# Attention scores of six tiles in one phase, values in one phase, and one score tile copied out of PSUM by VectorE

## The chip, the cores and the metric

The kernel runs on one core of a Trainium2 chip. The metric is the device time of one execution in microseconds (us); lower is better. The core has a matrix engine (TensorE; PE in the profile, with its weight loads listed apart as PEld), three engines for elementwise work (VectorE = DVE, ScalarE = ACT, GpSimd = POOL), a queue that issues the DMAs (SyncE = SP), a large on-chip memory (SBUF), and PSUM, the memory that matmuls write to. In this kernel PSUM is cut into three buffers of 128 x 1024 float32 (the pool `ps_2`) and two of 128 x 512 (`ps_1`).

## The reference, cut to what matters

```python
def _attn_ref(q, k, v):                      # batch 8, heads 12, sequence 448, head size 64
    scores = matmul(q, k.T) / sqrt(64) - log(448)
    attn = 1 / (1 + exp(-scores))            # a sigmoid, no softmax: no sum over a row
    return matmul(attn, v)

def _moe_ref(x, w_in, w_spatial, b_spatial, w_out):
    h = maximum(x @ w_in, 0);  u, g = halves of h
    g = (g - mean(g)) / sqrt(var(g) + 1e-6)
    g = einsum('ts,bsd->btd', w_spatial, g) + b_spatial
    return (u * g) @ w_out
```

Inputs and outputs are float32. The attention output of all heads, side by side, is `x`.

## The kernel before, in words

The eight batch elements are handled in four blocks of two (`m` = 0 to 3). A block first does the attention of its two batch elements, then the gated MLP: `gate_values` (tiles `pv`), `spatial` (`pg`), `gated` (`pu`) and `output` (`po`). The attention of the next block starts a little inside the MLP of the block before: its first four score tiles stand ahead of the last three `output` calls.

**Units and pairs.** A unit `(b, hp)` is one batch element and two heads; a block has 12 units, handled as six pairs (an even unit `n` and an odd unit `n + 1`). Two heads of 64 rows fill the 128 partitions, so every score or value step is two matmuls, one per head (`j` = 0, 1), in different halves of the matrix engine, which run at the same time. Keys are cut into three full tiles of 128 and one short tile of 64. A pair has seven score tiles: `evens` 0, 1, 2 (the even unit's full tiles), 3 (`NFULL`, the short tiles of both units in one), and `odds` 4, 5, 6 (the odd unit's).

**Scores** (`attention_scores`, tiles `psc`). A full tile is three products of split float32 numbers (`TERMS`: high by high, low by high, high by low), so six matmuls (L245; 64 rows by 128 columns of the engine). The short tile is done in plain float32 (L227; 64 by 64). Each `psc` takes one `ps_2` buffer; ScalarE applies the sigmoid on the way out of PSUM into SBUF (L253, tiles `at`). The high and low parts (`qks`) are made by `attention_splits` (L100 and L101): in block 0 the high part is made by ScalarE, later by VectorE; the low part always by VectorE. The very first pair (`direct`) is scored in plain float32, without splits.

**Values** (`attention_values`, tiles `pav`, one `ps_1` buffer per unit). For every `at` tile the product with `v` in plain float32 (L283): full tiles use 128 rows by 64 columns of the engine, the short tile 64 by 64, four matmuls for both units and both heads. When a unit is complete, ScalarE writes its high part to `x_s` (L289) and VectorE subtracts to get the low part (L262).

**The order of the work** is that in which the code is written: every engine executes its instructions in program order (`in_program_order`). For a pair inside a block, `attention` wrote: short tile of this pair; DMA loads; `evens` scores; values of the previous pair's `odds`; `odds` scores; splits of the next pair; values of this pair's `evens` and short tile.

**Weights.** In block 0 the float64 weights are loaded and converted between the attention steps. `load_weights(k)` runs k steps of the generator `weight_steps`: a DMA of a raw weight tile two tiles ahead (L159; `wraw`; up to the thirteenth in three buffers with the tag `tmp`), for the first spatial tile also a DMA of the bias (`b_bc`, L167), and VectorE work: three operations (L113, L124, L127), two (L129, L132), and a cast with a subtraction (L180, L181). A spatial weight tile (`w_sp`) needs the last two only. The loads of a raw tile wait until the buffer's earlier tile has been read, and they stand in SP's queue with the loads of q and k (L200, `raw`, three buffers) and of v (L205).

Of the kernel before, what the change touches and what calls it, by code (L numbers as in the profile page):

```python
# [8 lines left out]
F32 = mybir.dt.float32  # L9
F32R = mybir.dt.float32r  # L10
# [4 lines left out]
P = 128  # L15
# [20 lines left out]
def attn_gmlp_kernel(  # L36
# [25 lines left out]
    nc = tc.nc  # L62
# [138 lines left out]
        loaded[b, hp] = raw  # L201

    def value_loads(b, hp):
        vt = work.tile([P, 2 * NFULL + 1, P], F32, tag="v", name=f"v_{b}_{hp}", bufs=3)
        nc.sync.dma_start(vt, v[b, hp // 2])  # L205
        values[b, hp] = vt

# [2 lines left out]
    def attention_splits(b, hp):  # L210
        raw = loaded[b, hp][:, :PART]
        s = work.tile([P, 2, 2 * S], F32R, tag="split", name=f"qks_{b}_{hp}", bufs=3)[:, :, :PART]
        split(s[:, 0], s[:, 1], raw, nc.vector.tensor_copy if b > 1 else nc.scalar.copy)
        parts_of[b, hp] = s
# [2 lines left out]

    TILES = 2 * NFULL + 1

    def attention_scores(b, hp, t):  # L220
        psc = banks(f"psc_{b}_{hp}_{t}")
        if t == NFULL:
            for odd in range(2):
                raw = loaded[b, hp + odd]
                for j in range(2):
                    rows = slice(j * D, (j + 1) * D)
                    nc.tensor.matmul(  # L227
                        psc[odd * HALF : (odd + 1) * HALF, j, :S],
                        raw[rows, PART:],
                        raw[rows, FULL:PART],  # L230
                        start=True,
                        stop=True,
                    )
        else:
            unit = b, hp + t // (NFULL + 1)
            k = t % (NFULL + 1) * P
            if unit in parts_of:
                s = parts_of[unit]
                ops = [(s[:, a], s[:, e]) for a, e in TERMS]
            else:  # L240
                ops = [(loaded[unit], loaded[unit])]
            for i, (st, mv) in enumerate(ops):
                for j in range(2):
                    rows = slice(j * D, (j + 1) * D)
                    nc.tensor.matmul(  # L245
                        psc[:, j, :S],
                        st[rows, k : k + P],
                        mv[rows, FULL:PART],
                        start=i == 0,
                        stop=i == len(ops) - 1,  # L250
                    )
        at = work.tile([P, 2, 512], F32, tag="big", name=f"at_{b}_{hp}_{t}", bufs=7)[:, :, :S]
        nc.scalar.activation(at, psc[:, :, :S], AF.Sigmoid, bias=bias_s, scale=QK)  # L253
        return at

    pav_of = {}
# [4 lines left out]
        while late:  # L261
            nc.vector.tensor_sub(*late.pop(0))  # L262

    last = (NFULL, TILES - 1)

    def attention_values(b, hp, t, at):
        vt = values[b, hp]
        for odd in range(2):
            if t == NFULL:
                rows = slice(odd * HALF, (odd + 1) * HALF)  # L270
            elif (t > NFULL) == odd:
                rows = slice(0, P)
            else:
                continue
            unit = b, hp + odd
            start = t == odd * NFULL
            stop = t == last[odd]
            if start:
                pav_of[unit] = ps_1.tile([P, 512], F32, tag="ps1", name=f"pav_{b}_{hp + odd}")
            pav = pav_of[unit]  # L280
            for j in range(2):
                heads = slice(j * D, (j + 1) * D)
                nc.tensor.matmul(pav[heads, :S], vt[rows, t, heads], at[rows, j], start=start, stop=stop)  # L283
        for odd in range(2):
            if t == last[odd]:
                sl = slice((b % 2) * S, (b % 2 + 1) * S)
                x = x_s[:, :, hp + odd, sl]
                pav = pav_of.pop((b, hp + odd))[:, :S]
                nc.scalar.copy(x[:, 0], pav)  # L289
                late.append((x[:, 1], pav, x[:, 0].bitcast(F32)))  # L290
# [14 lines left out]
    def gate_values(m, ts):  # L305
# [26 lines left out]
            nc.vector.tensor_scalar_sub(rv[:, i], rv[:, i], mv[:, i, 0:1])  # L332
        load_weights(1)
        for i, t in enumerate(ts):
            vn = work.tile([P, 2, 512], F32R, tag="big", name=f"vn_{m}_{t}", bufs=7)
            if t != NFULL:
                parts = [(vn[:, 0], vn[:, 1], slice(0, P))]
            else:

                a, c = slice(0, HALF), slice(HALF, P)  # L340
                parts = [(vn[a, 0], vn[c, 0], a), (vn[c, 1], vn[a, 1], c)]
            for hi, lo, rows in parts:
                nc.vector.tensor_scalar_mul(hi, rv[rows, i], rstd[rows, i : i + 1])  # L343
                nc.vector.scalar_tensor_tensor(  # L344
                    lo,
                    rv[rows, i],
                    rstd[rows, i : i + 1],
                    hi.bitcast(F32),
                    op0=ALU.mult,
                    op1=ALU.subtract,  # L350
                )
            vns[t] = vn
            if t % 2 == 0:
                load_weights(1)
# [85 lines left out]
    def ahead(f, n, end=len(units)):  # L440
        if n < end:
            f(*units[n])
# [8 lines left out]
    def attention(m):  # L451

        first, end = 2 * NHP * m, 2 * NHP * (m + 1)
        ats = {}
        budget = [NYIELDS if m == 0 else 0]

        def weigh(n):
            n = min(n, budget[0])
            budget[0] -= n
            load_weights(n)  # L460

        def scores(n, ts):
            for t in ts:
                ats[n, t] = attention_scores(*units[n], t)

        def vals(n, ts):
            for t in ts:
                attention_values(*units[n], t, ats.pop((n, t)))
            late_splits()

        short, evens, odds = (NFULL,), tuple(range(NFULL)), tuple(range(NFULL + 1, TILES))
        for n in range(first, end, 2):
            direct = n == 0

            def loads():
                ahead(attention_loads, n + 3, end)
                ahead(value_loads, n + 2, end)
                ahead(attention_loads, n + 4, end)

            if direct:  # L480
                scores(n, evens + short)
            else:
                scores(n, short)
                loads()
                scores(n, evens)
            if n == first:
                yield
                if not direct:
                    attention_splits(*units[n + 1])
            else:  # L490
                vals(n - 2, odds)
                weigh(3)
            scores(n, odds)
            if direct:
                loads()
            ahead(attention_splits, n + 2, end)
            ahead(attention_splits, n + 3, end)
            vals(n, evens + short)
            weigh(3 + (n + 2 == end))
        vals(end - 2, odds)  # L500

    start_loads(0)
    load_weights(1)
# [84 lines left out]
```

## Time and profile before

| | |
|---|---|
| time, median of 3 runs | 692.84 us (692.56 to 693.68) |
| time of the profiled execution | 692.46 us |
| its span, first to last instruction | 690.7 us |
| TensorE busy | 680.6 us, 99% |
| VectorE busy | 282.1 us, 41% |
| ScalarE busy | 250.2 us, 36% |
| sigmoids (L253) | 168, mean 1008 ns |
| granted TensorE clock | 1.0 throughout |

How to read it: the span is cut by engine, busy time is the union of an engine's instructions. Matmuls overlap and their ends are modelled, so a matmul's length is not what it adds to the time; the distance between the starts of successive matmuls is. "The chain of waits" is the work that ended last, followed back from the end: each row has a start, a length, an engine and a line. A row of the timeline has start, length, engine, line, operation, tiles, and in brackets how long the engine had been idle and who ended that.

### The profile page before, as it was taken

The page shows a single profiled execution, that of the slowest core. Times are in us where ns is not written, and L with a number is a line of the kernel's source. Part 1 is how long each engine was busy: PE and PEld are TensorE (multiplying, and loading weights), DVE is VectorE, ACT ScalarE, POOL GpSimd, SP SyncE. Part 2 cuts the span into 40 slices and gives each one's busy share as a digit, 9 for nine tenths or more (in the row PEclk, how much of TensorE's full clock was granted, in tenths as well). Part 3 has the DMA queues.
Part 4 walks back from the last instruction along what each step waited for, and adds up shares of the span by engine and source line. Part 5 has one row for each costly group of instructions (what it writes and reads, how often), then busy time and mean ns, then how long its engine had stood idle before and what let it go on. Part 6 is the DMA issues. An engine that isn't in the chain of part 4 may idle for free.

```text
span 690.7 us, 8989 instructions
## 1 busy us (share of the span) xinstructions
PE 680.6 (99%) x3820; PEld 500.6 (72%) x3820; DVE 282.1 (41%) x448; ACT 250.2 (36%) x298; POOL 18.8 (3%) x36
## 2 busy tenths in 40 slices
PE   7999999999999999999999999999999999999997
PEld 3444788998745488999864458899985545889996
DVE  1999578903243237231224414622124341553020
ACT  6887122313467611011257751011136773101111
POOL 0000010000000001000000001100000000110000
PEclk9999999999999999999999999999999999999999
DMA  7683012422334200001332420000133410000102
GB/s 266 216 306 134 23 39 91 139 81 80 108 133 160 81 1 0 1 21 60 107 134 96 145 81 0 1 1 27 54 134 106 162 54 0 1 1 0 54 28 80
DMA packets 20248, 55.37 MB, mean 80 GB/s; under 512 B 1904, under 2 KB 8048, under 8 KB 20208
## 3 DMA queue, kind: packets, MB, share of 16 engines
q1 hardware_dynamic: 20208, 54.80, 22.9%
q8 instruction: 30, 0.49, 0.3%
q14 instruction: 10, 0.08, 0.0%
HBM read 43.78 MB, written 11.01 MB: 79 GB/s over the span
## 4 chain that ended last, share of the span: by engine, by line
PE 93%; DVE 5%; ACT 1%; DMA 0%; issue 0%; ACTq 0%
PE pav L283 20%; PE po L296 17%; PE pu L296 16%; PE psc L245 15%; PE pv L296 14%; PE pg L296 9%; PE psc L227 3%; DVE vn L344 1%; DVE stats L326 1%; ACT rv L322 1%; DVE wval L132 1%; DVE vn L343 0%; DMA raw<-qk_dram 0%; DVE wval L129 0%; DVE rv L332 0%
## 5 line engine op out<-in xcount | busy, mean ns | idle before, releaser
L253 ACT ACTIVATE at<-psc,bias_s 128x896 f32<-128x896 f32 x168 | 156.5, 1008 | 36.4 <-PE psc L227 25.3
L283 PE MATMUL pav<-at,v 128*64 128x448 f32 (+1 forms) x768 | 140.5, 551 | 0.0
L296 PE MATMUL po<-gs,w_out_s 128*128 128x448 f32 x576 | 120.1, 368 | 0.2
L296 PE MATMUL pu<-x_s,w_in_s 128*128 128x448 f32 x576 | 118.3, 365 | 1.4 <-DVE g L383 1.0
L296 PEld LDWEIGHTS po<-gs,w_out_s 128*128 128x128 f32 x576 | 107.8, 188 | 11.6 <-ACT at L253 1.2
L296 PEld LDWEIGHTS pu<-x_s,w_in_s 128*128 128x128 f32 x576 | 108.0, 188 | 10.7 <-DVE g L383 1.4
L296 PE MATMUL pv<-w_in_s,x_s 128*128 128x512 f32 x504 | 115.4, 390 | 0.0
L296 PEld LDWEIGHTS pv<-w_in_s,x_s 128*128 128x128 f32 x504 | 94.3, 188 | 22.3 <-issue 2.8
L245 PEld LDWEIGHTS psc<-qks 64*128 64x128 f32 x828 | 72.5, 184 | 39.2 <-ACT at L253 17.7
L283 PEld LDWEIGHTS pav<-at,v 128*64 128x64 f32 (+1 forms) x768 | 42.1, 135 | 78.0 <-issue 73.4
L245 PE MATMUL psc<-qks 64*128 64x448 f32 x828 | 97.6, 377 | 0.0
L262 DVE TENSOR_TENSOR x_s<-pav,x_s 128x448 fp32r<-128x448 f32 x48 | 30.0, 624 | 123.4 <-ACT x_s L289 123.4
L296 PE MATMUL pg<-w_sp_s,vn 128*128 128x448 f32 x352 | 72.8, 365 | 0.0
L296 PEld LDWEIGHTS pg<-w_sp_s,vn 128*128 128x128 f32 x352 | 66.0, 187 | 5.8
L406 DVE SCALAR_TENSOR_TENSOR g<-pu,g 128x896 f32<-128x896 f32 x16 | 17.5, 1091 | 123.8 <-PE pu L296 123.8
L435 ACT COPY osb<-po 128x896 f32<-128x896 f32 x24 | 21.8, 909 | 123.5 <-PE po L296 112.9
L101 DVE TENSOR_TENSOR qks<-raw,qks 128x832 fp32r<-128x832 f32 x46 | 46.7, 1026 | 14.3 <-ACT qks L100 13.1
L100 ACT CAST gs<-g 128x896 fp32r<-128x896 f32 x12 | 11.3, 944 | 100.0 <-DVE g L406 100.0
L289 ACT CAST x_s<-pav 128x448 fp32r<-128x448 f32 x48 | 25.6, 533 | 53.5 <-PE pav L283 53.1
L322 ACT ACTIVATE rv<-pv 128x1024 f32<-128x1024 f32 (+1 forms) x16 | 14.7, 917 | 81.3 <-PE pv L296 81.3
L326 DVE BATCH_NORM_STATS2 stats<-rv 128x6 f32<-128x512 f32 x28 | 19.0, 679 | 48.8 <-ACT rv L322 48.8
L100 DVE CAST qks<-raw 128x832 fp32r<-128x832 f32 x36 | 21.1, 587 | 35.5 <-PE po L296 35.3
(36 smaller groups left out, 239.1 us busy)
## 6 DMA issues: line engine op xcount, KB each, us to landing
raw<-qk_dram SPq DMA_DIRECT2D x48, 448.0 KB, 3.7
v<-v_dram SPq DMA_DIRECT2D x24, 448.0 KB, 4.3
out_dram<-osb SPq DMA_DIRECT2D x24, 448.0 KB, 2.6
wraw<-w_in_dram SPq DMA_DIRECT2D x12, 512.0 KB, 4.1
wraw<-w_out_dram SPq DMA_DIRECT2D x6, 512.0 KB, 3.8
wraw<-w_sp_dram SPq DMA_DIRECT2D x4, 256.0 KB, 4.4
b_bc<-b_sp_dram SPq DMA_DIRECT2D x1, 256.0 KB, 4.4
```

Source lines behind the costliest of these rows:

```text
L100: copy(hi, src)
L101: nc.vector.tensor_sub(lo, src, hi.bitcast(F32))
L227: nc.tensor.matmul(psc[odd * HALF : (odd + 1) * HALF, j, :S], raw[rows, PART:], raw[rows, FULL:PART], start=True, stop=True,)
L245: nc.tensor.matmul(psc[:, j, :S], st[rows, k : k + P], mv[rows, FULL:PART], start=i == 0, stop=i == len(ops) - 1,)
L253: nc.scalar.activation(at, psc[:, :, :S], AF.Sigmoid, bias=bias_s, scale=QK)
L262: nc.vector.tensor_sub(*late.pop(0))
L283: nc.tensor.matmul(pav[heads, :S], vt[rows, t, heads], at[rows, j], start=start, stop=stop)
L289: nc.scalar.copy(x[:, 0], pav)
L296: nc.tensor.matmul(ps, st, mv, start=start and i == 0, stop=stop and i == len(ops) - 1)
L322: nc.scalar.activation(rv[:, :n], pv[:, :n], AF.Relu)
L326: nc.vector.bn_stats(stats, rv[:, i])
L435: nc.scalar.copy(osb, po[:, :, :S])
```

## The change

Three things are written anew, all in the attention.

First, the order inside a pair. The six full score tiles now come in one phase, in the order 0, 1, 4, 2, 5, 6, followed by the short tile of the next pair; then all values of this pair come in one phase: short tile (both units), `evens`, `odds` (5, 6, 4). In a block after the first, the first pair's short tile and `evens` are still scored early, and its `odds` and the next pair's short tile follow after the `output` calls. Since the short tile now opens both units, `start` and `last` of the value sums change.

Second, in all pairs but a block's first, tile 4 (`by_copy`) is not passed through the sigmoid on its way out of PSUM: VectorE copies it to SBUF (L257 of the new file), and ScalarE applies the sigmoid in place there (L221), after the sigmoid of the next pair's short tile.

Third, what hangs on the order: DMA loads of q and k are issued one pair further ahead, `v` has two buffers for three, the `at` tiles have eight for seven, and the weight steps of block 0 are spread otherwise over the pairs (five per pair for six; four after the first pair for three; seven in the last).

TensorE, one pair in the middle of block 0 (`psc_4` and `pav_4` are even unit 4, `pav_5` odd unit 5, `psc_0` the next batch element's first). Before:

```order
L227 MATMUL psc_4_3_283<-raw_4_131 64x448 x2
L227 MATMUL psc_4_3_283<-raw_5_170 64x448 x2
L245 MATMUL psc_4_0_296<-qks_4_251 128x448 x6
L245 MATMUL psc_4_1_305<-qks_4_251 128x448 x6
L245 MATMUL psc_4_2_314<-qks_4_251 128x448 x6
L283 MATMUL pav_3_266<-at_2_4_231,v_2_129 64x448 x2
L283 MATMUL pav_3_266<-at_2_5_240,v_2_129 64x448 x2
L283 MATMUL pav_3_266<-at_2_6_249,v_2_129 64x448 x2
L245 MATMUL psc_4_4_339<-qks_5_254 128x448 x6
L245 MATMUL psc_4_5_348<-qks_5_254 128x448 x6
L245 MATMUL psc_4_6_357<-qks_5_254 128x448 x6
L283 MATMUL pav_4_372<-at_4_0_303,v_4_172 64x448 x2
```

The same pair now:

```order
L248 MATMUL psc_4_0_303<-qks_4_265 128x448 x6
L248 MATMUL psc_4_1_312<-qks_4_265 128x448 x6
L248 MATMUL psc_4_4_321<-qks_5_268 128x448 x6
L248 MATMUL psc_4_2_330<-qks_4_265 128x448 x6
L248 MATMUL psc_4_5_339<-qks_5_268 128x448 x6
L248 MATMUL psc_4_6_348<-qks_5_268 128x448 x6
L230 MATMUL psc_0_3_359<-raw_0_185 64x448 x2
L230 MATMUL psc_0_3_359<-raw_1_271 64x448 x2
L289 MATMUL pav_4_391<-at_4_3_248,v_4_241 64x448 x2
L289 MATMUL pav_5_394<-at_4_3_248,v_4_241 64x448 x2
L289 MATMUL pav_4_391<-at_4_0_310,v_4_241 64x448 x2
L289 MATMUL pav_4_391<-at_4_1_319,v_4_241 64x448 x2
```

The values that stood between `evens` and `odds` have moved behind all scores, and the short tile stands between the last full tile and the values.

SP's queue in block 0, from the load of unit 4 on (`raw` is q and k of a unit, `wraw` a raw weight tile, `b_bc` the bias). Before:

```order
L200 DMA raw_4_131<-qk_dram 128x896
L159 DMA wraw_153<-w_in_dram 128x1024
L200 DMA raw_5_170<-qk_dram 128x896
L205 DMA v_4_172<-v_dram 128x896
L200 DMA raw_0_174<-qk_dram 128x896
L159 DMA wraw_211<-w_sp_dram 128x512
L167 DMA b_bc<-b_sp_dram 128x512
```

Now:

```order
L200 DMA raw_4_129<-qk_dram 128x896
L205 DMA v_2_131<-v_dram 128x896
L159 DMA wraw_153<-w_in_dram 128x1024
L159 DMA wraw_171<-w_sp_dram 128x512
L167 DMA b_bc<-b_sp_dram 128x512
L200 DMA raw_5_183<-qk_dram 128x896
L200 DMA raw_0_185<-qk_dram 128x896
```

The second spatial weight tile and the bias now stand ahead of the load of unit 5.

VectorE in block 0, from the end of the first pair's even unit on (`x_s<-pav_0` and `pav_1` are the two units of the first pair). Before:

```order
L262 TENSOR_TENSOR x_s<-pav_0_139,x_s 128x448
L113 TENSOR_SCALAR wval_155<-wraw_86 128x512
L124 TENSOR_SCALAR wraw_86<-wraw_86 128x512
L127 TENSOR_SCALAR wraw_86<-wraw_86 128x512
L129 SCALAR_TENSOR_TENSOR wval_155<-wraw_86,wval_155 128x512
L132 SCALAR_TENSOR_TENSOR wval_155<-wraw_86,wval_155 128x512
L180 CAST w_in_s<-wval_155 128x512
L181 TENSOR_TENSOR w_in_s<-wval_155,w_in_s 128x512
L262 TENSOR_TENSOR x_s<-pav_1_148,x_s 128x448
L180 CAST w_sp_s<-wraw_88 128x512
L181 TENSOR_TENSOR w_sp_s<-wraw_88,w_sp_s 128x512
```

Now:

```order
L268 TENSOR_TENSOR x_s<-pav_0_139,x_s 128x448
L113 TENSOR_SCALAR wval_155<-wraw_86 128x512
L124 TENSOR_SCALAR wraw_86<-wraw_86 128x512
L127 TENSOR_SCALAR wraw_86<-wraw_86 128x512
L268 TENSOR_TENSOR x_s<-pav_1_142,x_s 128x448
L129 SCALAR_TENSOR_TENSOR wval_155<-wraw_86,wval_155 128x512
L132 SCALAR_TENSOR_TENSOR wval_155<-wraw_86,wval_155 128x512
L180 CAST w_in_s<-wval_155 128x512
L181 TENSOR_TENSOR w_in_s<-wval_155,w_in_s 128x512
L180 CAST w_sp_s<-wraw_88 128x512
L181 TENSOR_TENSOR w_sp_s<-wraw_88,w_sp_s 128x512
L257 COPY at_2_4_212<-psc_2_4_205 128x2x448
```

The second unit's subtraction now stands ahead of the first weight tile's last operations, and the copy of the second pair's tile 4 stands behind both weight tiles.

The diff:

```diff
--- before.py
+++ after.py
@@ -201,7 +201,7 @@
         loaded[b, hp] = raw
 
     def value_loads(b, hp):
-        vt = work.tile([P, 2 * NFULL + 1, P], F32, tag="v", name=f"v_{b}_{hp}", bufs=3)
+        vt = work.tile([P, 2 * NFULL + 1, P], F32, tag="v", name=f"v_{b}_{hp}", bufs=2)
         nc.sync.dma_start(vt, v[b, hp // 2])
         values[b, hp] = vt
 
@@ -217,7 +217,10 @@
 
     TILES = 2 * NFULL + 1
 
-    def attention_scores(b, hp, t):
+    def sigmoid(at, src):
+        nc.scalar.activation(at, src, AF.Sigmoid, bias=bias_s, scale=QK)
+
+    def attention_scores(b, hp, t, copied=False):
         psc = banks(f"psc_{b}_{hp}_{t}")
         if t == NFULL:
             for odd in range(2):
@@ -249,8 +252,11 @@
                         start=i == 0,
                         stop=i == len(ops) - 1,
                     )
-        at = work.tile([P, 2, 512], F32, tag="big", name=f"at_{b}_{hp}_{t}", bufs=7)[:, :, :S]
-        nc.scalar.activation(at, psc[:, :, :S], AF.Sigmoid, bias=bias_s, scale=QK)
+        at = work.tile([P, 2, 512], F32, tag="big", name=f"at_{b}_{hp}_{t}", bufs=8)[:, :, :S]
+        if copied:
+            nc.vector.tensor_copy(at, psc[:, :, :S])
+        else:
+            sigmoid(at, psc[:, :, :S])
         return at
 
     pav_of = {}
@@ -261,7 +267,7 @@
         while late:
             nc.vector.tensor_sub(*late.pop(0))
 
-    last = (NFULL, TILES - 1)
+    last = (NFULL - 1, NFULL + 1)
 
     def attention_values(b, hp, t, at):
         vt = values[b, hp]
@@ -273,7 +279,7 @@
             else:
                 continue
             unit = b, hp + odd
-            start = t == odd * NFULL
+            start = t == NFULL
             stop = t == last[odd]
             if start:
                 pav_of[unit] = ps_1.tile([P, 512], F32, tag="ps1", name=f"pav_{b}_{hp + odd}")
@@ -332,7 +338,7 @@
             nc.vector.tensor_scalar_sub(rv[:, i], rv[:, i], mv[:, i, 0:1])
         load_weights(1)
         for i, t in enumerate(ts):
-            vn = work.tile([P, 2, 512], F32R, tag="big", name=f"vn_{m}_{t}", bufs=7)
+            vn = work.tile([P, 2, 512], F32R, tag="big", name=f"vn_{m}_{t}", bufs=8)
             if t != NFULL:
                 parts = [(vn[:, 0], vn[:, 1], slice(0, P))]
             else:
@@ -468,36 +474,48 @@
                 attention_values(*units[n], t, ats.pop((n, t)))
             late_splits()
 
-        short, evens, odds = (NFULL,), tuple(range(NFULL)), tuple(range(NFULL + 1, TILES))
+        short, evens, odds = (NFULL,), tuple(range(NFULL)), (NFULL + 2, NFULL + 3, NFULL + 1)
+        by_copy = odds[-1]
         for n in range(first, end, 2):
             direct = n == 0
-
-            def loads():
-                ahead(attention_loads, n + 3, end)
-                ahead(value_loads, n + 2, end)
-                ahead(attention_loads, n + 4, end)
-
             if direct:
                 scores(n, evens + short)
+                ahead(attention_loads, n + 3, end)
+                scores(n, odds)
+                ahead(attention_loads, n + 4, end)
+            elif n == first:
+                scores(n, short + evens)
+                ahead(attention_loads, n + 3, end)
+                yield
+                attention_splits(*units[n + 1])
+                ahead(attention_loads, n + 4, end)
+                scores(n, odds)
             else:
-                scores(n, short)
-                loads()
-                scores(n, evens)
-            if n == first:
-                yield
-                if not direct:
-                    attention_splits(*units[n + 1])
-            else:
-                vals(n - 2, odds)
-                weigh(3)
-            scores(n, odds)
-            if direct:
-                loads()
+                scores(n, evens[:2])
+                ats[n, by_copy] = attention_scores(*units[n], by_copy, copied=True)
+                scores(n, evens[2:] + odds[:-1])
+            ahead(value_loads, n + 2, end)
+            if not direct and n + 2 < end:
+                scores(n + 2, short)
+            if not direct and n != first:
+                sigmoid(ats[n, by_copy], ats[n, by_copy])
+                weigh(4)
             ahead(attention_splits, n + 2, end)
             ahead(attention_splits, n + 3, end)
-            vals(n, evens + short)
-            weigh(3 + (n + 2 == end))
-        vals(end - 2, odds)
+
+            def loads():
+                ahead(attention_loads, n + 5, end)
+                ahead(attention_loads, n + 6, end)
+
+            if not direct:
+                loads()
+            vals(n, short + evens)
+            weigh(1 if n + 2 < end else 4)
+            vals(n, odds)
+            if direct:
+                weigh(3)
+                scores(n + 2, short)
+                loads()
 
     start_loads(0)
     load_weights(1)
```

## The prediction

> **What bounds the kernel now.** I read the page first, for who is busy and who is on the chain of waits:
>
> ```profile
> PE 680.6 (99%) x3820; PEld 500.6 (72%) x3820; DVE 282.1 (41%) x448; ACT 250.2 (36%) x298; POOL 18.8 (3%) x36
> PE 93%; DVE 5%; ACT 1%; DMA 0%; issue 0%; ACTq 0%
> ```
>
> TensorE is nearly never without a matmul, and 93% of the chain is TensorE's. So nothing is won by making another engine faster; time is won only where TensorE's own sequence gets shorter. Next the chain in order of time (start, length, engine, line), around the first pair, at the ends of the attention of blocks 0 and 1, and over one whole pair:
>
> ```profile
> 11.82 3.32 PE pav L283 x20
> ...
> 70.48 8.40 PE pv L296 x36
> ...
> 181.10 2.05 PE psc L245 x18
> ...
> 207.65 0.75 PE psc L227 x8
> 208.40 2.09 PE psc L245 x18
> 210.49 2.41 PE pav L283 x12
> 212.89 2.02 PE psc L245 x18
> 214.91 3.32 PE pav L283 x20
> 218.23 0.75 PE psc L227 x8
> ...
> 236.09 5.72 PE pav L283 x32
> 241.81 28.79 PE pv L296 x126
> ```
>
> A pair takes 0.75 + 2.09 + 2.41 + 2.02 + 3.32 = 10.59 us, with TensorE passing from one kind of matmul to another at each step. Third, the timeline inside one pair, for the distances between matmuls and for who releases whom:
>
> ```profile
> 212.35 0.55 PE L283 MATMUL pav<-at,v 128*64 128x448 f32 x2
> 212.82 2.09 PE L245 MATMUL psc<-qks 64*128 64x448 f32 x18
> 213.13 0.37 PE L245 MATMUL psc<-qks 64*128 64x448 f32 x2
> 213.80 2.80 ACT L253 ACTIVATE at<-psc,bias_s 128x896 f32<-128x896 f32 x3 [0.32 <-PE psc L245]
> 214.55 0.37 PE L245 MATMUL psc<-qks 64*128 64x448 f32 x2
> ```
>
> Two matmuls, one per head, start together; I call them a couple. 213.13 is the second couple of a score phase and 214.55 the ninth: 1.42 / 7 = 0.203 us per couple, 0.61 per full tile. Values and short tiles take 0.75 / 2 = 0.376 per couple (or per four of the short tile's).
>
> **What a change of phase costs.** From the last value couple to the first score couple are 0.47 us (212.35 to 212.82) where 0.376 is the rhythm, and to the second couple 0.31 where 0.203 is: an entry into scores costs 0.20. Entering values: 2.41 - 6 x 0.376 = 0.15. The short tile behind full ones: 3.32 - 8 x 0.376 - 0.15 = 0.16. The piece with 32 (evens, short, odds on end) holds three entries: 5.72 - 14 x 0.376 = 0.46. Only short scores behind short values cost nothing (0.75). So a pair has five entries, and what matters is the shape of the matmul, not its line. The first figure of a form such as 128*64 is the rows, the second the columns of the engine that it uses.
>
> **What the new order saves.** Per pair there remain: entering full scores (0.20), short scores behind full ones (not seen here between such forms; nearest row 0.16, bounds 0 and 0.20; I take 0.15), full values behind short ones (0.15). Short values behind short scores should be free, the mirror of what the chain shows. Without waits the pair is then: scores 2.02 + 9 x 0.203 = 3.85; short tile 0.90; values 14 x 0.376 + 0.15 = 5.41; together 10.16, so 0.43 less than 10.59.
>
> **What it adds: PSUM waits.** Before, three full tiles came in a phase and there are three `ps_2` buffers. Now six come, and from the fourth on TensorE waits for whoever empties a buffer. This already shows where a short tile and three full ones follow each other:
>
> ```profile
> 208.55 1.01 ACT L253 ACTIVATE at<-psc,bias_s 128x896 f32<-128x896 f32 x1 [0.34 <-PE psc L227]
> 209.61 0.50 PEld L245 LDWEIGHTS psc<-qks 64*128 64x128 f32 x6 [0.18 <-ACT at L253]
> 209.93 0.36 PE L245 MATMUL psc<-qks 64*128 64x448 f32 x2
> ```
>
> The sigmoid ends at 209.56, the waiting weight load starts at 209.61, and the tile's second couple starts at 209.93. So that couple comes no sooner than 0.37 after the sigmoid's end. In the timeline above the first sigmoid starts 0.98 after its tile's first couple (0.47 after its last) and three sigmoids take 2.80, one 1.01: a new one every 0.90. TensorE makes a tile in 0.61.
>
> Now I replay the six tiles from their first couple (0). Tile 0's sigmoid runs 0.98 to 1.99, tile 1's 1.88 to 2.88. The fourth tile (2) takes tile 0's buffer: second couple at 1.99 + 0.37 = 2.36, where undisturbed it would be at 0.31 + 9 x 0.203 = 2.14. Wait 0.22. The fifth (5) takes tile 1's: 2.88 + 0.37 = 3.25 instead of 2.36 + 0.61 = 2.97. Wait 0.28. The sixth (6) takes the buffer that VectorE copies out. No copy out of PSUM is in the trace; the nearest rows are
>
> ```profile
> L383 DVE TENSOR_TENSOR g<-pg,b_bc 128x896 f32<-128x896 f32 x16 | 17.4, 1088 | 20.0 <-PE pg L296 20.0
> L100 DVE CAST qks<-raw 128x832 fp32r<-128x832 f32 x36 | 21.1, 587 | 35.5 <-PE po L296 35.3
> ```
>
> I take 1.09, since L383 reads PSUM as the copy does; the cast, from SBUF, would give 0.63. The copy starts at 1.73 + 0.47 = 2.20, ends at 3.29, and lets the sixth tile's second couple go at 3.66, before its turn at 3.86. No wait by either price; a copy more than 0.20 late costs time. [...] The short tile's buffer (tile 2's, sigmoid to 4.04) is free before 4.36. So waits are 0.50 a pair, and the pair takes 10.66: 0.07 more than before. The saving is gone.
>
> [...]
>
> **A later block** (60.71 us before, 181.10 to 241.81): first odds 2.05, short tile 0.90, values 5.41; four pairs of 10.66; the last pair has no short tile behind it, 3.85 + 0.50 + values 5.56 (the short tile now behind full scores). Together 60.91, +0.2; three blocks +0.6.
>
> **Block 0** (58.66 before, 11.82 to 70.48): values 5.56, short tile 0.90, a first pair of 10.66 + 0.14 (one buffer still holds the short tile), three of 10.66, the last 9.91: 59.15, +0.5. But here two queues have moved. In the timeline of before VectorE, SP and ScalarE did, among other things,
>
> ```profile
> 15.18 0.53 ACT L289 CAST x_s<-pav 128x448 fp32r<-128x448 f32 x1 [0.45 <-PE pav L283]
> 15.86 0.62 DVE L262 TENSOR_TENSOR x_s<-pav,x_s 128x448 fp32r<-128x448 f32 x1
> 17.77 0.69 DVE L129 SCALAR_TENSOR_TENSOR wval<-wraw,wval 128x512 uint32<-128x512 uint32 x1
> 18.50 0.69 DVE L132 SCALAR_TENSOR_TENSOR wval<-wraw,wval 128x512 uint32<-128x512 uint32 x1
> 19.22 0.33 SPq L159 DMA_DIRECT2D wraw<-w_sp_dram  x1
> 19.22 0.43 DVE L180 CAST w_in_s<-wval 128x512 fp32r<-128x512 f32 x1
> 19.59 0.43 SPq L167 DMA_DIRECT2D b_bc<-b_sp_dram  x1
> 19.68 0.69 DVE L181 TENSOR_TENSOR w_in_s<-wval,w_in_s 128x512 fp32r<-128x512 f32 x1
> ```
>
> and the loads of q and k landed, by the list of DMA issues (median from issue to landing, from 14 to 24 us and from 28 to 60 us), after
>
> ```profile
> raw<-qk_dram SPq DMA_DIRECT2D x2, 448.0 KB, 4.1
> raw<-qk_dram SPq DMA_DIRECT2D x5, 448.0 KB, 4.8
> ```
>
> The load of the second spatial weight (19.22) waits for L132's end (19.19), as its buffer is the first raw tile's. The load of unit 5 now stands behind it. The second unit's values end at 11.82 + 5.56 = 17.4, ScalarE's cast at 18.0, VectorE's subtraction, now ahead of L129, at 18.6, L129 and L132 (0.73 and 0.69) at 20.0. SP issues the weight at 20.0, the bias at 20.4, unit 5 at 20.9. Landing takes 4.1 to 4.8; I take 4.8, the crowded stretch, as two others were issued just before: 25.7. TensorE wants unit 5 for the next short tile, at 11.82 + 5.56 + 0.90 + 3.85 + 0.64 = 22.8. **Stall 2.9 us, once.** Were the load in time, the copy would still be late: it stands behind the last steps of both weight tiles (19.22 to 20.37 for one), 20.0 + 2 x 1.15 = 22.3, ends at 23.4, and the sixth tile's second couple comes at 23.8 for 22.3. Bounds: 1.5, and 3.6 if the two loads ahead cost it another 0.7, the difference of the two rows. Later pairs of block 0 have less at stake. The buffer of a load is free when a split is done, by these two groups:
>
> ```profile
> L100 ACT CAST qks<-raw 128x832 fp32r<-128x832 f32 x10 | 8.4, 896 | 0.0
> L101 DVE TENSOR_TENSOR qks<-raw,qks 128x832 fp32r<-128x832 f32 x46 | 46.7, 1026 | 14.3 <-ACT qks L100 13.1
> ```
>
> ScalarE's last sigmoid of the pair ends at 7.6 (tile 2's starts at 3.03, four more follow at 0.90, 1.01 long), the cast at 8.5, the low part at 9.5; the load lands at 14.3, which is 3.7 into the next pair, where it is wanted at 4.4.
>
> **The sum.** 0.6 + 0.5 + 2.9 = +4.0. The profiled execution took 692.46 (span 690.7 and 1.8 around it), so 696.5; the median of the three runs is 0.38 above it: **696.8**. The first loads, the MLP and the end are not touched and get nothing.
>
> **Rivals.**
> 1. *No stall in block 0* (unit 5 in time, the copy not late): +1.1, 693.9, no measurable change: 0.2% (1.4 us) is about what a measurement of this kernel can tell. For it: landings were hidden before. Against: two queued items ahead of the load. 0.2.
> 2. *Faster: two engines empty PSUM as fast as TensorE fills it*, no waits. Then a later block takes 60.91 - 2.50 = 58.41 (-2.3) and block 0, without its 0.14 too, -2.1 + 2.9: -6.1, so 686.7; without the stall 683.8. Decided by the fourth and fifth tile: below 0.43 of waits per pair the change gains. For it: 0.22 and 0.28 are small. Against: both tiles wait for ScalarE, which VectorE's copy doesn't relieve in time. 0.13.
> 3. *VectorE falls behind in all of block 0*:
>
> ```profile
> 28.56:39.15 10.59, 10.59 (x79) 5.21 (x80) 9.94 (x19) 9.14 (x12) 0.00 (x0) 1.00 0.77 262
> 210.49:221.07 10.58, 10.58 (x78) 5.20 (x80) 4.30 (x6) 7.57 (x10) 0.00 (x0) 1.00 0.38 134
> ```
>
> The third figure with a count is VectorE's: 9.94 of 10.59 in block 0, 4.30 later. The copy adds 1.09; five weight steps for six take away some 1.1 to 1.4. It should just fit; if each of the four later pairs loses 1 us, 700.8. 0.15.
>
> The change does do what it says: the order of the instructions shows it.
>
> **Chances.** Forecast 0.52, rivals 0.2, 0.13, 0.15. The forecast's own range is 694.5 to 699 (stall 1.5 to 3.6, waits 0.45 to 0.58 over 20 pairs). From 692.6 to 700.5 lies all but the second rival and the end of the third. Faster 0.14 (the second rival and a little of the first), same 0.17 (most of the first), slower 0.69.
>
> **What would show it.** Right: in the waits, TensorE's weight loads of scores wait for the sigmoid twice per pair, 0.2 to 0.3 each; a later pair takes 10.6 to 10.7; a hole of 2 to 3 us before 26 us, ended by the load of q and k. Wrong: a pair of 10.2 without those waits, waits for VectorE's copy in later blocks, or a block 0 that stays behind by more than 4 us.

## The result and the profile after

The changed kernel is slower: 699.18 us median of 4 runs (697.17 to 701.9), the kernel before beside it 692.83; the ratio is 1.0092, interval [1.0077, 1.0108]. A second series of five runs gave 697.43 (697.17 to 697.75) with 692.76 for before, ratio 1.0068 [1.0054, 1.0082]. Over both series seven executions lie between 697.17 and 697.80; the two others (700.57 and 701.9) have a mean granted clock of 0.997 where these have 0.999 or 1.0. That is a matter of its own, below. The profiled execution took 697.8, its span 696.0, 5.3 more than before.

The page of the changed kernel, busy times and the chain of waits by engine:

```profile
PE 683.1 (98%) x3820; PEld 502.6 (72%) x3820; DVE 303.8 (44%) x468; ACT 250.6 (36%) x298; POOL 18.8 (3%) x36
PE 91%; DVE 5%; ACT 1%; DMA 1%; issue 1%; ACTq 0%
```

VectorE has 22 us more to do (the copies) and is no nearer to being the bound. New is the 1% of DMA in the chain: a transfer that TensorE waits for in the middle of the work. The chain in order of time shows where (start, length, engine, line; L248 full score tiles, L230 short tiles, L289 values, L302 the MLP):

```profile
13.03 5.57 PE pav L289 x32
...
22.09 5.13 DMA raw<-qk_dram
...
38.93 5.41 PE pav L289 x32
...
49.55 5.41 PE pav L289 x32
...
75.45 8.40 PE pv L302 x36
...
186.08 2.05 PE psc L248 x18
...
205.13 2.83 PE psc L248 x24
...
215.79 2.77 PE psc L248 x24
...
246.86 28.79 PE pv L302 x126
```

Block 0 goes from 13.03 to 75.45: 62.42 for 58.66, +3.76. A later block, 186.08 to 246.86: 60.78 for 60.71; the three later blocks together lose 0.35. The pair from 205.13 to 215.79 is 10.66; the twelve pairs of the later blocks that can be read off in this way take 10.60 to 10.68, 10.64 on the mean. The rest of the 5.3 lies ahead of the first values (13.03 for 11.82, +1.21), where TensorE does the same work in both kernels. Over the profiled executions of this study these values start anywhere from 11.18 to 13.03, and in a second profile of the changed kernel at 12.15. In the traces of both kernels the first couples there follow each other at 0.75 us, later ones at 0.376, while the column of the granted clock reads 1.0; the step between the two comes at about 8 us in the kernel before and at about 10 in the changed one. In the chains of eight other profiles the first twelve matmuls take from 4.01 us (values at 11.18) to 4.85 and the twelve ahead of the values 2.46 in all of them, so the moment of the step differs there too. So most of the +1.21 at least is spread, not the change.

The stall, in the timeline of the changed kernel (start, length, engine or queue, line, operation, and in brackets the idle time and who ended it):

```profile
20.47 0.69 DVE L132 SCALAR_TENSOR_TENSOR wval<-wraw,wval 128x512 uint32<-128x512 uint32 x1
21.19 0.33 SPq L159 DMA_DIRECT2D wraw<-w_sp_dram  x1
21.56 0.43 SPq L167 DMA_DIRECT2D b_bc<-b_sp_dram  x1
22.09 1.71 SPq L200 DMA_DIRECT2D raw<-qk_dram  x2
23.33 1.08 DVE L257 COPY at<-psc 128x896 f32<-128x896 f32 x1
24.47 0.87 PE L248 MATMUL psc<-qks 64*128 64x448 f32 x6 [1.13 <-DVE at L257]
27.27 0.59 PE L230 MATMUL psc<-raw 64*64 64x448 f32 x2 [1.02 <-DMA raw<-qk_dram]
```

L132 ends, the weight is issued, the bias behind it, then unit 5; it lands 5.13 us later and TensorE goes on at 27.27. Here are two waits one behind the other: the sixth tile for VectorE's late copy, then the short tile for the load.

And the waits of a later pair, in the timeline of the same kernel:

```profile
217.69 0.50 PEld L248 LDWEIGHTS psc<-qks 64*128 64x128 f32 x6 [0.26 <-ACT at L221]
217.85 1.09 DVE L257 COPY at<-psc 128x896 f32<-128x896 f32 x1 [0.82 <-PE psc L248]
218.59 1.11 PEld L248 LDWEIGHTS psc<-qks 64*128 64x128 f32 x12 [0.39 <-ACT at L221]
```

The weight loads of the fourth and the fifth tile are released by a sigmoid; the sixth tile's follows the fifth's without a stop (x12), so the copy was in time.

### The profile page after: what moved, and what is told of

The parts are those of the page before. It is cut to its first block, busy times and chain, and to the rows that moved or that the text cites. A ratio compares the mean times of both kernels' runs of the same rounds, so it can differ in the third digit from the quotient of the medians.

```text
span 696.0 us, 8981 instructions
## 1 busy us (share of the span) xinstructions
PE 683.1 (98%) x3820; PEld 502.6 (72%) x3820; DVE 303.8 (44%) x468; ACT 250.6 (36%) x298; POOL 18.8 (3%) x36
## 3 DMA queue, kind: packets, MB, share of 16 engines
HBM read 43.78 MB, written 11.01 MB: 79 GB/s over the span
## 4 chain that ended last, share of the span: by engine, by line
PE 91%; DVE 5%; ACT 1%; DMA 1%; issue 1%; ACTq 0%
PE pav L289 19%; PE po L302 17%; PE pu L302 16%; PE psc L248 14%; PE pv L302 14%; PE pg L302 9%; PE psc L230 3%; DMA raw<-qk_dram 1%; DVE vn L350 1%; DVE stats L332 1%; ACT at L221 1%; ACT rv L328 1%; DVE wval L132 0%; DVE vn L349 0%; DVE wval L129 0%
## 5 line engine op out<-in xcount | busy, mean ns | idle before, releaser
L221 ACT ACTIVATE at<-psc,bias_s 128x896 f32<-128x896 f32 x148 | 138.8, 1006 | 35.3 <-PE psc L230 21.5
L289 PE MATMUL pav<-at,v 128*64 128x448 f32 (+1 forms) x768 | 135.2, 543 | 0.0
L302 PE MATMUL po<-gs,w_out_s 128*128 128x448 f32 x576 | 120.1, 368 | 0.2
L302 PE MATMUL pu<-x_s,w_in_s 128*128 128x448 f32 x576 | 118.3, 365 | 1.5 <-DVE g L389 1.0
L302 PEld LDWEIGHTS po<-gs,w_out_s 128*128 128x128 f32 x576 | 107.8, 188 | 11.6 <-ACT at L221 1.2
L302 PEld LDWEIGHTS pu<-x_s,w_in_s 128*128 128x128 f32 x576 | 108.0, 188 | 10.7 <-DVE g L389 1.4
L302 PE MATMUL pv<-w_in_s,x_s 128*128 128x512 f32 x504 | 115.4, 390 | 0.0
L302 PEld LDWEIGHTS pv<-w_in_s,x_s 128*128 128x128 f32 x504 | 94.3, 188 | 22.3 <-issue 2.8
L289 PEld LDWEIGHTS pav<-at,v 128*64 128x64 f32 (+1 forms) x768 | 46.2, 136 | 83.1 <-issue 79.8
L248 PE MATMUL psc<-qks 64*128 64x448 f32 x828 | 100.2, 379 | 1.7 <-DVE at L257 1.1
L248 PEld LDWEIGHTS psc<-qks 64*128 64x128 f32 x828 | 72.4, 184 | 36.8 <-issue 16.4
L302 PE MATMUL pg<-w_sp_s,vn 128*128 128x448 f32 x352 | 72.8, 365 | 0.0
L302 PEld LDWEIGHTS pg<-w_sp_s,vn 128*128 128x128 f32 x352 | 66.0, 187 | 5.8
```

The costliest lines, as they stand in the source:

```text
L221: nc.scalar.activation(at, src, AF.Sigmoid, bias=bias_s, scale=QK)
L248: nc.tensor.matmul(psc[:, j, :S], st[rows, k : k + P], mv[rows, FULL:PART], start=i == 0, stop=i == len(ops) - 1,)
L302: nc.tensor.matmul(ps, st, mv, start=start and i == 0, stop=stop and i == len(ops) - 1)
```

## The experiments

The theory is that of the prediction: entries saved (0.43 a pair), given back as two PSUM waits (0.50 a pair), and one stall in block 0. The rivals are that no stall matters, that the waits are something else, or that another limit of TensorE sets a pair's 10.6. Line numbers of the experiments are shifted by some lines.

**The load ahead of the weight steps.** In the first pair, and nothing else:

```diff
             if direct:
-                weigh(3)
                 scores(n + 2, short)
                 loads()
+                weigh(3)
```

> The changed kernel with one edit in the very first pair: the loads of q and k of units 5 and 6 are issued ahead of its weight steps. My theory: the 3.3 us by which TensorE is late in the second pair of block 0 comes from the load of unit 5 behind the second spatial weight tile in SP's queue (its landing ended the wait at 27.3 us), and behind that lies the late copy of tile 4 (sixth tile at 24.5 us, short tile possible at 25.3). So block 0, from the first values to the first pv, falls from 62.4 to about 60.4 us, no wait for q and k is left there, and the time is about 695.5. Rival: VectorE, with the copy on top of the weights, is what holds block 0 back; then nothing changes, since VectorE does the same work in the same order. On the clock: if the hole of 3 us is also what makes the granted clock dip in some executions (0.997 in two of four, 3 us longer), every execution now shows 0.999 or 1.0 and the runs lie within 1 us; if dips are chance, they stay.

694.93 us (694.07 to 695.48, 6 runs), ratio 1.0027 [1.0016, 1.0038]. The chain of waits of this run:

```profile
12.04 5.60 PE pav L289 x32
...
22.42 1.01 DVE at L257
...
72.46 2.76 PE pv L302 x11
```

The load is gone from the chain, the copy has taken its place: block 0 is 60.42, 2.0 less than in the changed kernel. What was expected of the clock did not come: two of the six executions show 0.998, and they lie 1.4 us apart.

**And two weight steps for three behind the loads** (`weigh(2)`), so that VectorE reaches the copy earlier.

> As the kernel before it, and also one weight step less ahead of the second pair (three, as before the change, for four), so that VectorE's copy stands behind one weight tile and not two. My theory: the copy comes 1.06 us earlier (about 22.3 us), the sixth tile waits 0.3 us instead of 1.3, block 0 takes about 59.4 us and the time is about 694.5. Rival (the load alone counted): the same time as the kernel before it, 695.5. Rival (VectorE's total work binds block 0): the step left out comes back later in the block, so nothing is gained over the changed kernel.

694.18 us (693.4 to 694.68, 11 runs), ratio 1.0014 [1.0005, 1.0023]. The chain of waits:

```profile
12.46 5.60 PE pav L289 x32
...
21.78 1.01 DVE at L257
...
71.85 3.21 PE pv L302 x13
```

Block 0 is 59.39, for 59.15 forecast without a stall. So the stall was 3.0 of the 3.76, and 697.43 - 694.18 = 3.25 us of the time (3.5, if each is counted from the kernel before beside it, 692.76 and 693.04). What is left over before is the 1.1 forecast for this case (693.9).

**The copy as the second tile** in blocks 1 to 3, so that the fifth tile waits for VectorE instead of ScalarE's second sigmoid:

```diff
+                early = 1 if m else 2
-                scores(n, evens[:2])
+                scores(n, evens[:early])
                 ats[n, by_copy] = attention_scores(*units[n], by_copy, copied=True)
-                scores(n, evens[2:] + odds[:-1])
+                scores(n, evens[early:] + odds[:-1])
```

> The changed kernel with tile 4 scored and copied second instead of third in the pairs of blocks 1 to 3 (0, 4, 1, 2, 5, 6). My theory: the fourth and fifth score tiles wait for ScalarE, one tile every 0.90 us. With the copy second, the fifth tile takes the copied buffer: copy from 1.59 to 2.68 after the first couple, second couple at 3.05 where 2.97 would be its turn, so 0.08 instead of 0.28; the fourth still waits 0.22. A pair falls from 10.61 to 10.41, a later block from 60.8 to 59.8, the time by 3.0, to about 694.5 (without a dip of the clock). Rival: the waits belong to six tiles in one phase as such (weight loads, the number of buffers), not to who empties which; then nothing changes.

696.4 us (693.95 to 698.0, 6 runs), ratio 1.0047 [1.0032, 1.0062]. The chain of waits over one pair:

```profile
195.87 4.09 PE psc L248 x36
...
206.35 4.09 PE psc L248 x36
```

A pair is 10.48 for 10.64 (10.41 expected): which engine empties which tile is worth 0.16 a pair, as the theory has it. The time was 1.9 above the expectation. Of this the profiled execution shows 1.7 in block 0 (64.14 us for 62.42), which this edit leaves as it was: the load was issued 10.1 us after the first values for 9.1, and landed after 5.84 us for 5.13. Two of the six executions had a clock of 0.996.

**No copy**: ScalarE's sigmoid empties the third tile as well (`attention_scores` without `copied`, and no second sigmoid).

> The changed kernel without VectorE's copy: ScalarE applies the sigmoid to tile 4 out of PSUM like to the others, in the order 0, 1, 4, 2, 5, 6. My theory: the sixth tile now waits for tile 4's sigmoid (2.78 to 3.79 after the first couple, second couple at 4.16 for 3.86, 0.30) and the short tile 0.1 more; a pair rises by 0.4, a later block by 1.9, block 0 by about 1.3 (its second pair is covered by the load of unit 5): about 704.5 without a dip of the clock. Rival (the copy does nothing, TensorE waits for the first two sigmoids alone): the same time as the changed kernel, or up to 1.5 less, since VectorE is freed of it.

707.14 us (703.96 to 707.72, 4 runs), ratio 1.0195 [1.0178, 1.0213]. The chain of waits of one pair:

```profile
192.12 5.41 PE pav L289 x32
...
203.18 5.41 PE pav L289 x32
```

A pair is 11.06 (11.01 expected): VectorE's copy does save 0.4 a pair, against a chain of sigmoids alone. The waits grow as the emptying does. The 2.6 us more than expected led to the clock: in this run's table by stretches (from:to, length, busy times of PE, PEld, DVE, ACT and POOL with counts, then the granted clock, DMA share, GB/s), the clock falls behind the stall.

```profile
28.00:30.00 2.00, 2.00 (x10) 0.53 (x6) 0.00 (x0) 1.62 (x2) 0.00 (x0) 0.51 0.87 351
30.00:32.00 2.00, 2.00 (x8) 0.61 (x6) 1.81 (x2) 0.95 (x2) 0.00 (x0) 0.64 0.11 43
```

Counted as if the clock were either whole or half (0.50 is the lowest in any run's table), 0.51 over 2 us and 0.64 over 2 us make (0.49 + 0.36) x 2 / 0.5 = 3.4 us at half. The value phase of that stretch took 6.99 us for 5.41.

**Two engines on one tile.** In blocks 1 to 3 the tiles 0, 1 and 4 are emptied half by each engine; block 0 is as with two weight steps above. The main part of the edit (the values of these tiles also move behind those of the others):

```diff
+        if copied == "half":
+            sigmoid(at[:, 0], psc[:, 0, :S])
+            nc.vector.tensor_copy(at[:, 1], psc[:, 1, :S])
```

> In blocks 1 to 3 the three tiles that the fourth, fifth and sixth tile wait for are each emptied by two engines, one head by ScalarE's sigmoid and the other by VectorE's copy at the same time; their second sigmoid comes later in place. Block 0 has the three steps and the early load of the run with three weight steps. Theory (the waits of a later pair are the time to empty tiles 0 and 1 with one engine): no PSUM waits are left in blocks 1 to 3, a pair takes 10.16 us, a block 58.4 instead of 60.8, so 694.2 - 3 x 2.4 = 687 us. Rival (six tiles in a row are too many for the two engines however the work is divided, or the more instructions of ScalarE make new waits): a pair stays at 10.6, 694 us or more.

694.67 us (694.16 to 695.55, 6 runs), ratio 1.003 [1.0019, 1.0042]. By the numbers the rival won, but the edit did not do what it says. The timeline of a pair:

```profile
191.56 1.85 ACT L221 ACTIVATE at<-psc,bias_s 128x448 f32<-128x448 f32 x3 [0.33 <-PE psc L248]
192.22 1.84 DVE L258 COPY at<-psc 128x448 f32<-128x448 f32 x3 [0.34 <-ACT at L221]
192.90 1.72 PEld L248 LDWEIGHTS psc<-qks 64*128 64x128 f32 x18 [0.61 <-DVE at L258]
```

Three halves take 1.85 and 1.84, but VectorE's first starts only when ScalarE's first is done (191.56 + 0.64 = 192.20): it waits for ScalarE's sigmoid of the other half, and a pair later again (202.91, behind 202.24 + 0.64). The two instructions read one PSUM tile and write one `at` tile; which of the two makes the program put them in order, this run does not show. The weight load that waits for the first tile so starts 1.34 after the sigmoid (192.90 - 191.56), later than behind one whole sigmoid of 1.01, and a pair of block 1 takes 10.66 to 10.69, as before. So this run tells nothing of the rival, and the next one was made for it.

**Half of the emptying left out** in blocks 1 to 3 of the changed kernel. The first two sigmoids and the copy read one head only, and a constant stands in place of the other:

```diff
-        if copied:
+        if copied and b > 1:
+            nc.gpsimd.memset(at[:, 1], 0.0)
+            nc.vector.tensor_copy(at[:, 0], psc[:, 0, :S])
+        elif copied:
             nc.vector.tensor_copy(at, psc[:, :, :S])
+        elif b > 1 and t < 2:
+            nc.gpsimd.memset(at[:, 1], 0.5)
+            sigmoid(at[:, 0], psc[:, 0, :S])
```

> The changed kernel, but in blocks 1 to 3 the first two sigmoids and the copy of a pair read one head of the PSUM tile and leave the other out (GpSimd writes a constant in its place): they take about 0.63 us for 1.01 and 1.09, with everything else as in the changed kernel. Theory (a later pair is 10.16 us of TensorE's work and 0.50 of waits for the fourth and fifth tile): no PSUM waits, a pair of 10.16 to 10.2, a block of 58.4 to 58.6, 2.3 us less for each of three, so about 690.5 us beside 697.4. Rival (the waits are only what the profile shows of another limit: TensorE takes 10.6 for a pair in this order anyway): pair 10.6, 697 us.

691.34 us (689.54 to 693.96, 12 runs), ratio 0.9974 [0.9962, 0.9986]; the eight executions with a clock of 0.999 or more have a median of 690.5. The chain of waits:

```profile
187.24 2.04 PE psc L248 x18
...
205.79 3.83 PE psc L248 x36
...
215.97 3.83 PE psc L248 x36
...
245.74 28.83 PE pv L308 x126
```

A pair is 10.18, a block 58.50: the waits are the emptying of PSUM, 10.64 - 10.18 = 0.46 of a pair, and the order by itself is worth what was forecast (10.59 - 10.18 = 0.41 for 0.43).

Block 0 of this run is that of the changed kernel, and the profiled execution, with a clock of 0.997, shows what can lengthen its stall:

```profile
11.18 5.60 PE pav L295 x32
...
19.71 1.36 SPq L167
...
21.17 5.70 DMA raw<-qk_dram
...
28.33 6.61 PE pav L295 x30
...
76.69 8.42 PE pv L308 x36
```

SP spent 1.36 us on issuing the bias, for 0.43 in the changed kernel's profile; so unit 5's load was issued 10.0 us after the first values for 9.1, and it landed after 5.70. Behind the stall the clock was at half for 3.4 us (worked out at the end of this text), and the value phase took 6.61 for 5.41. Block 0 took 65.51, 3.1 more than 62.42. In the profile of the run with two weight steps the bias took 1.01 us, and in those of the runs with the copy second and without a copy unit 5's load was issued late as well, 10.1 and 10.3 us after the first values (22.78 - 12.68 and 21.86 - 11.56); why the bias takes longer in some executions is not known.

**The stall filled.** The changed kernel with throwaway matmuls ahead of the short tile that waits:

> The changed kernel with 24 throwaway matmuls (six quadruples of 0.376 us, 2.3 us) just before the short tile that waits for unit 5's load in block 0. Nothing else changes, and the output is the same. Theory (the hole before 27.3 us is what lets the granted clock fall in some executions): every execution takes 697 to 698.5 us with a mean granted clock of 0.999 or more, and none 700 or more. Rival (the fall of the clock has nothing to do with the hole): the same spread as the changed kernel beside it, about half of the executions at 0.997 and 700 to 702 us.

699.74 us (698.88 to 700.22, 4 runs), ratio 1.01 [1.0087, 1.0114], a clock of 1.0 in all four. The timeline:

```profile
24.38 4.74 PE L230 MATMUL psc<-raw 64*64 64x448 f32 x48
```

The filling was twice as long as meant, and ended after the load had landed: hence 2 us more than expected. The clock did stay up. But in the changed kernel beside it, it did too:

> The changed kernel once more, beside the one with the filled hole and on the same chip. Both theories: some executions at 697 to 698 us with a clock of 0.999 or 1.0, and some, about half, at 700 to 702 us with 0.997. If all of them are at 697 to 698, the chip makes the difference, and the filled hole tells nothing.

697.43 us, all five with 0.999 or 1.0. As said there, the pair of runs tells nothing of the clock.

**A longer stall.** The other direction: three more weight steps (`weigh(6)` for `weigh(3)`) ahead of the short tile and the load, and so also ahead of VectorE's copy.

> The changed kernel with three more weight steps ahead of the short tile and the loads behind the first pair (six for three), so that unit 5's load is issued later still and the hole before it grows by 2 to 4 us. Theory (a hole makes the granted clock fall to half for some 3.4 us in executions where it fills enough of some stretch, so a longer one does it in all): mean granted clock 0.998 or less in all or nearly all executions, and 2 to 3 us on top of the longer hole: 701 to 704 us. Rival (the fall comes by chance, with or without a hole): 699.5 to 701 us, with a clock of 0.999 or 1.0 in most.

700.92 us (700.04 to 702.17, 4 runs), ratio 1.0111 [1.0098, 1.0124], a clock of 0.994 in all four. The table by stretches of this run, then the end of the stall in its timeline:

```profile
26.00:28.00 2.00, 0.24 (x2) 0.24 (x4) 1.99 (x3) 0.00 (x0) 0.00 (x0) 0.61 0.99 344
28.00:30.00 2.00, 2.00 (x8) 0.36 (x10) 1.90 (x5) 0.00 (x0) 0.00 (x0) 0.50 1.03 418
30.00:32.00 2.00, 2.00 (x12) 0.47 (x4) 1.86 (x5) 0.84 (x1) 0.00 (x0) 0.50 1.04 413
32.00:34.00 2.00, 2.00 (x8) 0.57 (x8) 0.77 (x2) 2.00 (x4) 0.00 (x0) 0.69 0.18 70
```

```profile
27.76 2.55 PE L230 MATMUL psc<-raw 64*64 64x448 f32 x6 [3.95 <-DVE at L257]
```

The clock is at half for (0.39 + 0.50 + 0.50 + 0.31) x 2 / 0.5 = 6.8 us, twice the 3.4 of the run without the copy. The idle time of 3.95 us was ended by VectorE's copy, not by the load. By the clock the theory holds: it fell in all four executions. Which stall is enough is taken up at the end of this text. The time came out within the rival's range, 0.1 below the theory's; some 1.3 of these 6.8 us (half clock from about 26.4 on, the first matmul at 27.76) were still spent waiting.

**A version of both.** Block 0 in the order of the kernel before, blocks 1 to 3 in the new order with the copy second:

```diff
+        for n in range(first, end, 2) if m == 0 else ():
+            odds = tuple(range(NFULL + 1, TILES))
...
+        for n in range(first, end, 2) if m else ():
...
-                scores(n, evens[:2])
+                scores(n, evens[:1])
                 ats[n, by_copy] = attention_scores(*units[n], by_copy, copied=True)
-                scores(n, evens[2:] + odds[:-1])
+                scores(n, evens[1:] + odds[:-1])
```

> Block 0 keeps the order of the kernel before (two score phases and two value phases per pair, no copy); blocks 1 to 3 have the new order with VectorE's copy as the second tile. Theory (all that the change costs lies in block 0's first pair and in PSUM waits, and what it saves are entries): block 0 58.7 us as before, a later pair 10.48 and a later block 59.95 us as measured in the run with the copy second, so 692.8 - 3 x 0.76 = 690.5 us, faster than both kernels. Rival (part of the loss of block 0 lies outside it, or the gain of the later blocks hangs on how block 0 ended): 692 us or more.

690.41 us (689.55 to 690.48, 5 runs), ratio 0.9955 [0.9943, 0.9967]: faster than both kernels, and 0.1 from the sum. The chain of waits:

```profile
11.28 3.32 PE pav L289 x20
...
69.64 8.40 PE pv L302 x36
...
180.68 2.05 PE psc L248 x18
...
189.06 4.10 PE psc L248 x36
...
199.54 4.11 PE psc L248 x36
...
240.68 28.79 PE pv L302 x126
```

Block 0 is 58.36, a later pair 10.48 and a later block 60.00.

## Why the prediction was right

The forecast was 696.8 from one execution's sum, slower, with 692.6 to 700.5 around it; the executions with a clock of 0.999 or 1.0 take 697.2 to 697.8. The first median, 699.18, lies inside that range but 2.4 above the forecast, and just outside the 694.5 to 699 that the prediction gave for its own mechanism. That the sum came so close is in part luck: block 0 lost 3.76 for 3.4 and the later blocks 0.35 for 0.6, two misses that cancel (4.1 for 4.0). By its steps:

- **What a pair saves.** Forecast 0.43 (10.59 to 10.16). Right: 10.18 with the waits taken away, 0.41.
- **The PSUM waits.** Forecast 0.50, at the fourth and fifth tile, none at the sixth. Right in place and nearly in size: 0.46 (10.64 for 10.66 forecast). The copy took 1.08 to 1.09 (all 20 of them), the value taken from the row of L383.
- **A later block.** Forecast +0.2 each, measured +0.1: 0.02 a pair less.
- **The stall.** Forecast 2.9, of which 1.5 would remain as the copy's if the load were in time. The mechanism was right: the load stands behind L132, the weight and the bias, and the late copy lies behind it. Counted from the first values, SP issues the load at +9.1 (20.9 - 11.82 in the forecast, 22.09 - 13.03 in the trace). That it fits to the tenth holds for the two profiles in which the bias's issue takes 0.43 (this one, and 21.20 - 12.13 with the stall filled); in three other profiles with the same queue the load came at +10.0 to +10.3. The landing was undersized: 4.8 taken, 5.13 in the profiled execution, 5.70 and 5.84 in two others. The stall was 3.0 by block 0, and 3.25 to 3.5 by the times. With the load early the late copy remained, as forecast: 60.42 - 59.15 = 1.3 for the 1.5.
- **The rivals.** No stall: the runs with the load ahead gave 694.2 and 694.9 for the 693.9 worked out, but it was not the case here. Two engines that empty as fast as TensorE fills: its price was right (58.50 a block for 58.41), its condition not met. VectorE behind in all of block 0: the pairs behind the first run as in later blocks, 10.62 from 38.93 to 49.55, and block 0 without the stall is 59.39.
- **What no step had**: a load issued later than counted, and a fall of the granted clock, which the sum leaves out. They are the likely reason for the changed kernel's two executions above 700 us, and with them for the first median: the run with half of the emptying left out has the same block 0, the same mean clock of 0.997 in its profiled execution, and there 3.1 us more in block 0. That is argued and not shown, as no profile of those two executions was kept.

The gain that the change was able to have is thus accounted for: 0.41 a pair from fewer entries, 0.46 a pair given back to waits, and block 0 made worse once.

## What to carry to other kernels

Before merging two short phases into a long one, replay the buffers: from the first tile beyond their number on, the rate was here that of the engines that empty them (ScalarE one in 0.90 us, where TensorE makes one in 0.61), and it matters which engine holds which tile (0.16 a pair here for exchanging two). A step that is moved takes its DMA issues with it; count what stands ahead of them in the queue, one item at a time, and leave room for an item that takes longer: the count came out to the tenth in two profiles with this queue, and was 0.9 to 1.2 us too short in three others. Where stages have different limits, try the new order by stage: the old order in block 0 and the new one elsewhere beat both.

## What the runs showed of the hardware

In three profiles the granted clock fell in or behind a stall of TensorE, for 3.4, 3.4 and 6.8 us at half speed (the runs without a copy, with half of the emptying left out, and with the longer stall). Which stall is enough has no sharp edge here. The timelines of three executions, the wait that ended last (the run with half of the emptying left out, the run with the copy second, the changed kernel again):

```profile
26.92 0.67 PE L230 MATMUL psc<-raw 64*64 64x448 f32 x2 [2.52 <-DMA raw<-qk_dram]
```

```profile
28.66 0.59 PE L230 MATMUL psc<-raw 64*64 64x448 f32 x2 [2.77 <-DMA raw<-qk_dram]
```

```profile
26.46 0.59 PE L230 MATMUL psc<-raw 64*64 64x448 f32 x2 [1.10 <-DMA raw<-qk_dram]
```

With 2.52 of idle time (each of the three has some 1.1 more about 2 us ahead of it) the clock fell (its table has 0.83, 0.50 and 0.82 over the three stretches of 2 us from 26 to 32, again 3.4 us at half), with 2.77 it did not (1.00 in every stretch from 20 to 36), with 1.10 it did not (a mean of 0.999, for 0.997 with 2.52), with 3.49 in the run without a copy it fell for 3.4, with 3.95 it fell for 6.8. So the length of the idle time alone does not decide it here: 2.52 was enough once and 2.77 once was not. What else decides it is not shown. Nor is it shown that the two executions of the changed kernel with 0.997 had a longer stall than the profiled one, as no trace of them exists; that the load's issue (9.1 to 10.3 us after the first values) and its landing (5.13 to 5.84) vary is.

Also new: an engine's copy and another's sigmoid of two halves of one PSUM tile did not run side by side in this program, though they read different heads: VectorE's copy started at 192.22, released by the end of ScalarE's sigmoid (192.20). Separate tiles for the two heads were not tried.
